# Rounds of 512 columns for Q, K and V in a recurrent segment loop, with the heads laid out anew and longer rows for the streamed weights

## The chip, the cores and the metric

The kernel runs on one core of one Trainium2 chip. The metric is the device time of the whole program in microseconds, as the median of repeated runs. The kernel before took 1744.48 us, the median of three runs between 1734.66 and 1751.12.

A core has several engines that run their own instruction lists side by side and wait for each other by semaphores: TensorE (PE) multiplies matrices, VectorE (DVE) and ScalarE (ACT) copy and compute element by element, GpSimd (POOL) does a few odd jobs, and SyncE (SP) only issues DMA transfers here. PE's results land in PSUM and have to be copied from there to the main on-chip memory (SBUF) before PE can use them again.

## The reference

Two attention layers read sequences of 2048 tokens with 640 features, and a gate mixes their results. Layer A goes through the sequence in 64 segments of 32 tokens. Eight memory rows are put in front of each segment, and the first eight rows of a segment's result are the memory of the next one, so the segments can't run side by side.

```python
n_seg = S // seg_len                      # 2048 / 32 = 64
L = M + seg_len                           # 8 + 32 = 40
mask = (idx[:, None] < M) | (idx[:, None] >= idx[None, :])
mem = mem0
for s in range(n_seg):
    xs = x[:, s * seg_len:(s + 1) * seg_len, :].copy()
    h = jnp.concatenate([mem, xs], axis=1)            # 40 x 640
    q = jnp.einsum('btd,dhe->bhte', h, Wq)            # 32 heads of 192
    k = jnp.einsum('btd,dhe->bhte', h, Wk)
    v = jnp.einsum('btd,dhe->bhte', h, Wv)
    scores = jnp.einsum('bhqe,bhke->bhqk', q, k) * scale
    scores = jnp.where(mask[None, None], scores, -1000000000.0)
    p = _softmax(scores, axis=-1)
    o = jnp.einsum('bhqk,bhke->bhqe', p, v)
    o = jnp.einsum('bhte,hed->btd', o, Wo)
    mem = o[:, :M, :].copy()
    outs.append(o[:, M:, :])
```

Layer B is a local attention of 32 heads of 20 features, in which each position sees eight positions at distances 0, 2, ... 14. The result is `g * a + (1 - g) * b` with `g = sigmoid(x . gate_w)`. All data are bfloat16. The four weights of A have 640 x 6144 elements each, 7.9 MB, 31.5 MB in all; they are read again in each segment, and not all of them fit in SBUF.

## The kernel before

**Stages.** Layer B comes first (0 to about 178 us of the span); its result lies in DRAM until it is mixed in. A pre-pass follows (178 to 357 us): the last eight rows of each segment depend on no memory, so Q, K and V of these 512 rows (called z in the code) are computed for all segments at once (`project_qk`, four passes p = 0 to 3: two of Q, two of K; then `project_v`) and stored in `zpk_dram`. The segment loop (357 to 1689 us) then has 32 rows per segment: eight memory rows and 24 rows of x. A tail, `part_z` (1689 to 1747 us), multiplies the z rows of all segments by Wo.

**One segment.** `hT` holds the segment's 640 features in five chunks (`kc`) of 128 partitions, by 32 rows. PE has 128 columns of output partitions, and a matmul with 32 rows uses a strip of 32 of them, so four matmuls run at once, one in each strip j. Such four make a quad. Of the 6144 columns of Wq a round R takes 1536, four strips of 384 columns, and accumulates over kc: five quads a round, four rounds each of Q, K and V, 60 quads in all (L736 for Q and K, L838 for V).

- `m_qk(i, kcs)` issues the quads of round i, where even i are Q and odd i are K. `c_qk(i)` copies the round from PSUM to a staging slot `V[i % 4]` of the tile TZ: on ACT, but on DVE for i = 7 (L745).
- `t_qk(i)` transposes a round on PE, three transposes of 128 columns (L754), and `c_t(i)` copies them out with DVE (L761): Q into the tile ZB (`QTa`), K into free slots of ZB and TZ (`kt_runs`). One such slot shares its columns of ZB with `a4`, the tile from which the segment's result is stored to `out_dram`.
- The heads are handled in two halves h. `s_a` and `s_b` compute scores (L785, L794), `e_exp`, `e_mask`, `e_norm` and `e_recip` are the softmax: exps on ACT (four a half, L803), the mask, a matmul with `bones` that gives the sums (L817), Ln and Exp(-x) on ACT and two products on DVE.
- `m_v(R, kcs)` and `c_v(R)` project V and copy it (L845; round 1 on DVE, the others on ACT).
- `pv_half(h)` is P V, 48 small matmuls per half (L861, L866); copies on ACT and DVE bring the result of the x rows to SBUF (L872), and `c_z` the z rows (L881).
- `o_group(part, i2)` is the output projection, twelve quads for columns 0 to 383 (`oa`) and twelve for 384 to 639 (`ob`), all L902. ACT copies the sum to `whi` (L987 for `oa`, L995 for `ob`). `sel` picks the eight memory rows out of it by small matmuls (L912), and DVE writes them into the next segment's `hT` (L915). `tail` mixes in layer B's rows, which a DMA has brought to `a4`, and `store` sends `a4` to `out_dram`.

**Order.** Within the loop the instructions of PE, ACT and DVE run in the order in which the code issues them (`tc.manual_schedule`). DMAs are issued on two queues: SP's carries all weights, ACT's the segment's small loads and stores (`load_z`, `load_vz`, `load_seg`, a4, `out_dram`, `oz_dram`), between ACT's own instructions. So a DMA that waits on a queue holds up what stands behind it.

**Weights.** They are cut into 80 slices of 384 KB (128 partitions x 1536 columns): a slice of Q, K or V is one (round, kc). 66 slices are loaded once, during layer B, the pre-pass and the first segment (`wres`, `wlate`), and stay in SBUF. 14 are read again in each segment by SP into five buffers (`wstream`, tile `wst`); `weights_setup` picks them from a list of times so that their uses are spread over the segment, Q, K, V and the output part alike. The slices of Wq, Wk and Wv come from the input tensors in rows of 3072 bytes; three of the output's come from a copy in DRAM, `wscr`.

Of the kernel before, what the change touches and what calls it, by code (L numbers as in the profile page):

```python
# [10 lines left out]
BF = mybir.dt.bfloat16  # L11
# [3 lines left out]
N_STREAM = 14  # L15
N_EARLY = 20
# [4 lines left out]
WBUFS = 5  # L21
# [6 lines left out]
class _K:  # L28
# [463 lines left out]
    def slice_keys(self):  # L492
        keys = []
        for R in range(4):
            keys += [("q", R, kc) for kc in range(self.KC)] + [("k", R, kc) for kc in range(self.KC)]
        for R in range(4):
            keys += [("v", R, kc) for kc in range(self.KC)]
        keys += [("oa", i) for i in range(12)] + [("ob", i) for i in range(8)]
        return keys

    def slice_info(self, key):

        if key[0] in ("oa", "ob"):
            Wov = self.Wo.rearrange("(c p) f -> p c f", p=128)
            n, f0, f1 = (4, 0, 384) if key[0] == "oa" else (6, 384, 640)
            return Wov[:, n * key[1]:n * key[1] + n, f0:f1], (n, f1 - f0)
        W = {"q": self.Wq, "k": self.Wk, "v": self.Wv}[key[0]].rearrange("(c p) f -> p c f", p=128)
        return W[:, key[2], key[1] * 1536:(key[1] + 1) * 1536], None

    def weights_setup(self):  # L510
        nc, tc = self.nc, self.tc
        keys = self.slice_keys()
        gap = {("q", 0, 0): 300, ("k", 0, 1): 160, ("k", 0, 3): 70, ("q", 2, 2): 900, ("v", 0, 0): 1700, ("v", 2, 0): 800,
               ("v", 3, 0): 550, ("oa", 0): 150, ("oa", 6): 1200}
        at, t = {}, 0
        for k in keys:
            t += gap.get(k, 0)
            at[k] = t
            t += 163
        self.stream_keys = set()  # L520
        for i in range(N_STREAM):
            left = [k for k in keys if k not in self.stream_keys]
            self.stream_keys.add(min(left, key=lambda k: abs(at[k] - (i + 0.5) * t / N_STREAM)))
        rest = [k for k in keys if k not in self.stream_keys]
        use = [(m, R) for m in "qkv" for R in range(4)]
# [23 lines left out]
    def load_slice(self, pool, key, name, tag=None, t=None):  # L549
        src = self.slice_info(key)[0]  # L550
        if t is None:
            t = pool.tile([128, 1536], BF, name=name, **({"tag": tag} if tag else {}))
            self.load_slice(pool, key, name, tag, t)
            return self.slice_view(key, t)
# [574 lines left out]
```

## Time and profile before

| | before |
|---|---|
| median of three runs | 1744.48 us |
| profiled execution | 1748.69 us, its span 1747.0 us |
| mean granted PE clock | 0.983 |
| segment, mean of 64 | 20.74 us |
| DMA over the span | 477.57 MB, 273 GB/s; queue q1 (weights) 415.76 MB, q10 (ACT's) 56.46 MB, q8 (instructions) 4.75 MB |
| wst loads, 384 KB each | 325 from Wv, 260 from Wk, 192 from wscr, 130 from Wq |

The profile shows one execution. "Busy" is the time in which an engine worked on an instruction; PE is its matmuls, PEld its weight loads, which run beside them. A line such as "L745 ACT CAST TZ<-ps_qk 128x384 bf16<-128x384 f32 x448 | 208.0, 479" is a group of equal instructions: source line, engine, operation, destination and source with partitions x elements and type, how many there were, the busy time of all in us and the mean of one in ns. After the second bar stands the engine's idle time just ahead of them, and what ended most of it. In the chain of waits, the work that ended last is followed back from the end, each step to what released it; "issue" there is time in which the engine waited for nothing that the profile shows. In the timeline a row has the start and the length in us, the engine, line, operation and count, and in brackets the idle time ahead of it.

### The profile page before, as it was taken

To read this page: it belongs to the slowest core of one execution; us is meant where nothing else is said; L and a number is where in the kernel's file an instruction comes from. 1 tells how busy PE (TensorE), PEld (TensorE's weight loads), DVE (VectorE), ACT (ScalarE), POOL (GpSimd) and SP (SyncE) were. 2 spreads that over 40 slices of the span, in tenths; PEclk is the share of its full clock that TensorE was granted. 3 is DMA by queue.
4 is the path that set the end of the run, shared out by engine and by line. 5 is a ranking of instruction groups with operands and counts; after the bars stand their busy time and mean duration, and the time that the engine had idled before them with its cause. 6 is when DMAs were issued, how large, how long until landed. Compare 5 with 4: busy or idle time off the path is not lost.

```text
span 1747.0 us, 83365 instructions
## 1 busy us (share of the span) xinstructions
PE 1603.0 (92%) x37049; PEld 1012.7 (58%) x37049; DVE 632.1 (36%) x2095; ACT 873.1 (50%) x2338; POOL 60.0 (3%) x124
## 2 busy tenths in 40 slices
PE   7887999889999999999998999999999999999989
PEld 4544544356565566666665666666665566666657
DVE  3765333233333333333333333333333333333320
ACT  3887322245554455555554555545555555555550
POOL 2030000000000000000000000000000000000000
PEclk9998899999999999999999999999999999999999
DMA  7897895989898898899998888988998888888881
GB/s 198 210 238 172 277 270 162 267 277 307 291 297 282 279 295 288 296 305 306 309 292 274 288 292 300 303 287 292 310 306 295 294 295 299 291 292 291 297 280 31
DMA packets 299702, 477.57 MB, mean 273 GB/s; under 512 B 100172, under 2 KB 176460, under 8 KB 299340
## 3 DMA queue, kind: packets, MB, share of 16 engines
q1 hardware_dynamic: 200208, 415.76, 73.4%
q10 hardware_dynamic: 99132, 56.46, 11.1%
q8 instruction: 290, 4.75, 1.1%
q14 instruction: 72, 0.59, 0.1%
HBM read 430.40 MB, written 44.48 MB: 272 GB/s over the span
## 4 chain that ended last, share of the span: by engine, by line
PE 74%; ACT 9%; DMA 8%; issue 5%; ACTq 2%; DVE 1%; SPq 1%; DVEq 0%
PE ps_qk L736 23%; PE ps_v L838 10%; PE ps_wo L902 9%; PE ps_pre L603 6%; PE ps_qkT L754 5%; PE ps_S L785 4%; PE ps_oT L861 3%; PE ps_z L1060 3%; PE ps_pre L617 3%; DMA out_dram<-ZB 2%; ACT TZ L845 2%; PE ps_bqk L234 2%; ACT ZB L987 2%; ACT TZ L872 1%; PE ps_mem L912 1%
## 5 line engine op out<-in xcount | busy, mean ns | idle before, releaser
L736 PEld LDWEIGHTS <-hT 128*32 128x32 bf16 x10240 | 265.7, 96 | 156.0 <-issue 19.8
L745 ACT CAST TZ<-ps_qk 128x384 bf16<-128x384 f32 x448 | 208.0, 479 | 270.8 <-PE ps_qk L736 267.7
L736 PE MATMUL ps_qk<-wres_q,hT 128*32 128x384 bf16 x4608 | 259.5, 329 | 5.0 <-issue 3.3
L736 PE MATMUL ps_qk<-wlate_k,hT 128*32 128x384 bf16 x3584 | 235.3, 327 | 2.2 <-issue 1.8
L838 PE MATMUL ps_v<-wlate_v,hT 128*32 128x384 bf16 x3840 | 208.8, 329 | 0.2 <-issue 0.2
L902 PEld LDWEIGHTS <-TZ 128*32 128x32 bf16 x6144 | 160.1, 97 | 81.8 <-issue 42.0
L761 DVE COPY ZB<-ps_qkT 128x384 bf16<-128x384 bf16 x256 | 90.6, 354 | 212.5 <-PE ps_qkT L754 212.5
L902 PE MATMUL ps_wo<-wlate_oa,TZ 128*32 128x384 bf16 x2560 | 150.2, 333 | 11.8 <-issue 10.7
L838 PEld LDWEIGHTS <-hT 128*32 128x32 bf16 x5120 | 114.9, 96 | 65.7 <-issue 7.7
L902 PE MATMUL ps_wo<-wlate_ob,TZ 128*32 128x256 bf16 x2688 | 129.0, 279 | 14.3 <-issue 14.2
L736 PE MATMUL ps_qk<-wst,hT 128*32 128x384 bf16 x1536 | 132.6, 328 | 4.4 <-issue 3.3
L803 ACT ACTIVATE TZ<-ps_S 32x224 bf16<-32x224 f32 x256 | 89.0, 348 | 75.5 <-PE ps_S L794 71.4
L838 PE MATMUL ps_v<-wst,hT 128*32 128x384 bf16 x1280 | 108.7, 329 | 6.3 <-DMA wst<-in_A_Wv_dram 6.3
L872 DVE CAST TZ<-ps_oT 128x192 bf16<-128x192 f32 x256 | 79.4, 351 | 83.8 <-PE ps_oT L866 83.7
L803 ACT ACTIVATE ZB<-ps_S 32x224 bf16<-32x224 f32 x256 | 89.0, 348 | 38.8 <-PE ps_S L794 36.6
L872 ACT CAST TZ<-ps_oT 128x192 bf16<-128x192 f32 x256 | 69.6, 327 | 76.8 <-PE ps_oT L866 76.8
L754 PE MATMUL ps_qkT<-ident,TZ 128*128 128x128 bf16 x1536 | 107.7, 219 | 0.1
L915 DVE CAST hT<-ps_mem 128x24 bf16<-128x24 f32 x126 | 22.5, 179 | 223.4 <-PE ps_mem L912 223.4
L845 ACT CAST TZ<-ps_v 128x384 bf16<-128x384 f32 x192 | 92.4, 481 | 17.4 <-PE ps_v L838 15.7
L754 PEld LDWEIGHTS <-TZ 128*128 128x128 bf16 x1536 | 88.7, 98 | 20.6 <-issue 20.6
L861 PEld LDWEIGHTS <-TZ 32*128 32x128 bf16 (+1 forms) x4096 | 48.1, 97 | 75.6 <-issue 27.0
L713 POOL COPY TZ<-ZB 128x384 bf16<-128x384 bf16 x64 | 32.6, 510 | 1515.2 <-DMA ZB<-zpk_dram 717.0
(139 smaller groups left out, 2312.9 us busy)
## 6 DMA issues: line engine op xcount, KB each, us to landing
wst<-in_A_Wv_dram SPq DMA_DIRECT2D x325, 384.0 KB
wst<-in_A_Wk_dram SPq DMA_DIRECT2D x260, 384.0 KB
wst<-wscr SPq DMA_DIRECT2D x192, 384.0 KB
wst<-in_A_Wq_dram SPq DMA_DIRECT2D x130, 384.0 KB
zpk_dram<-ZS ACTq DMA_DIRECT2D x4, 3072.0 KB
ZB<-zpk_dram ACTq DMA_DIRECT2D x64, 192.0 KB
wres_q<-in_A_Wq_dram SPq DMA_DIRECT2D x18, 384.0 KB
zpk_dram<-ZV ACTq DMA_DIRECT2D x32, 192.0 KB
```

The source lines that it names most:

```text
L603: nc.tensor.matmul(ps[:], lhsT=sls[r][kc][:, c0:c0 + 128], rhs=zTi[:, kc, :], start=(kc == 0), stop=(kc == KC - 1))
L736: nc.tensor.matmul(pq[32 * j:32 * j + 32, 0:384], lhsT=hT[:, kc, :], rhs=sl[:, 384 * j:384 * j + 384], start=(kc == 0), stop=(kc == KC - 1 ...
L745: cp(sts[i], pqs[i][:, 0:384])
L754: nc.tensor.transpose(pT[:, t, :, :, :].rearrange("p j b i -> p (j b i)"), st[:, 128 * t:128 * t + 128], self.ident[:])
L761: nc.vector.tensor_copy(q_blocks(R)[:, 1:5, :, :].rearrange("p b c i -> p c b i"), pT.rearrange("p t j b i -> p (t j) b i"))
L785: nc.tensor.matmul(grid(h, par)[:, :, 0:80].rearrange("p j (b r i) -> p j b r i", r=2, i=8)[:, :, :, r, :], lhsT=KTs[R][t][k0:k1, :], rhs= ...
L803: nc.scalar.activation(E[ps], pSs[h][ps, :, 112 * j:112 * j + 112], ACT.Exp, scale=scale_a)
L838: nc.tensor.matmul(pvs[R][32 * j:32 * j + 32, 0:384], lhsT=hT[:, kc, :], rhs=sl[:, 384 * j:384 * j + 384], start=(kc == 0), stop=(kc == KC ...
L845: cp(V[R], pvs[R][:, 0:384])
L861: nc.tensor.matmul(out[:, r, t, :], lhsT=V[2 * h + r][ks, f0:f1], rhs=E[ks, par, 0:80].rearrange("p (b r i) -> p b r i", r=2, i=8)[:, :, r ...
L872: cps[j % 2](oTxs[2 * h + j // 2][:, 6 * (j % 2):6 * (j % 2) + 6, :], pos[j][:, 0:240].rearrange("p (c q) -> p c q", q=40)[:, :, 8:40])
L902: nc.tensor.matmul(pso[part][32 * jj:32 * jj + 32, 0:n], lhsT=oTxs[2 * (R // 2) + j // 2][:, 6 * (j % 2) + 3 * (R % 2) + t, :], rhs=o_weig ...
```

## The change

Q, K and V go in three rounds u of 512 columns per strip instead of four of 384. The heads are laid out so that strip J holds the same eight heads in all rounds: the 1536 columns from 1536 J on, in twelve chunks of 128. A resident tile is now one (matrix, strip J, kc) with the rounds that are not streamed (`units`, `tile_of`, `res`). A streamed unit is one (matrix, round, kc) for all four strips: 128 partitions x 2048 columns, 512 KB, of which eleven are listed by hand (`STREAM`): four of Q, three of K and four of V, none of the output part. All of them are copied to `wscr` in DRAM first, four on SP's queue in layer B (`N_COPY`), seven at the start of the third pass of `project_qk`, and are read from there in rows of 4096 bytes, into four buffers.

In the loop there are 45 quads of 512 columns instead of 60 of 384, and the sum of copies falls: six of Q and K on ACT, three of V, all on DVE. A fourth staging slot, the new tile XB, and new slots for transposed K (`k_runs`) follow from the new shape; none of these shares columns with `a4` any more. Transposes are 24 a segment as before, four a round. The copies of transposed Q and K are split where a round crosses the two halves of heads (`parts`). The softmax's reciprocal is in two pieces (`e_recip_a` on ACT, `e_recip_b` on DVE), P V's copies are their own step (`c_x`), and the order of the steps from the first normalisation to the output is new. `o_group` goes through the chunks in a new order, `order`, such that the first six groups need only the first half of heads; the six groups that remain of each part are issued without interleaving. The load of `a4` is issued after the second P V's copies instead of before the first output group. In the tail, `load_oz` brings each fourth of the data in two halves into tiles that hold two rounds, and `sort_oz` sorts it from there.

The diff, cut to what is named here:

```diff
-N_STREAM = 14
-N_EARLY = 20
+STREAM = (("q", 0, 1), ("k", 0, 0), ("q", 0, 3), ("k", 0, 3), ("q", 2, 0), ("q", 2, 4), ("k", 2, 1), ("v", 0, 0),
+          ("v", 0, 3), ("v", 1, 1), ("v", 1, 4))
+N_EARLY = 25
+N_COPY = 4
...
-WBUFS = 5
+WBUFS = 4
...
+    def units(self, m, kc):
+        return [u for u in range(3) if (m, u, kc) not in STREAM]
...
+        self.wscr = dict(zip(STREAM, self.dram.tile([len(STREAM), 128, 2048], BF, name="wscr")))
...
+    def res(self, m, J, kc, c0, n):
+        f0 = 512 * self.units(m, kc).index(c0 // 512) + c0 % 512
+        return self.res_tiles[m, J, kc][:, f0:f0 + n]
+
+    def load_unit(self, key):
+
+        m, u, kc = key
+        t = self.wstream.tile([128, 2048], BF, name="wst", tag="wst")
+        self.nc.sync.dma_start(t[:].rearrange("p (j f) -> p j f", j=4), self.unit_src(key))
+        return t
+
+    def unit_src(self, key):
+        m, u, kc = key
+        return self.W[m][:, kc, :].rearrange("p (j f) -> p j f", j=4)[:, :, 512 * u:512 * u + 512]
+
+    def copy_unit(self, key):
+        self.nc.sync.dma_start(self.wscr[key].rearrange("p (j f) -> p j f", j=4), self.unit_src(key))
+
+    def get_unit(self, key):
+        if key in self.ahead:
+            return self.ahead.pop(key)
+        t = self.wstream.tile([128, 2048], BF, name="wst", tag="wst")
+        self.nc.sync.dma_start(t[:], self.wscr[key])
+        return t
...
+        loads = [lambda k=k: self.load_res(k, self.tile_of(self.wres, k)) for k in self.early]
+        self.pre_q = {}
+        loads += [lambda k=k: self.pre_q.update({k: self.load_unit(k)})
+                  for k in sorted(STREAM, key=lambda k: k[1]) if k[0] == "q"]
+        loads += [lambda k=k: self.copy_unit(k) for k in STREAM[:N_COPY]]
...
+            sts = {k: self.pre_q[k] if m == "q" else self.load_unit(k) for k in STREAM if k[0] == m and k[1] == 2 * Rp}
...
+            if p == 2:
+                for k in STREAM[N_COPY:]:
+                    self.copy_unit(k)
...
+        def load_v(J):
+            t = self.wstream.tile([128, 2048], BF, name="wst", tag="wst")
+            for x, (m, u, kc) in enumerate(vkeys):
+                nc.sync.dma_start(t[:, 512 * x:512 * x + 512],
+                                  self.W["v"][:, kc, 1536 * J + 512 * u:1536 * J + 512 * u + 512])
+            return t
...
+        for k in STREAM[:WBUFS]:
+            self.ahead[k] = self.get_unit(k)
...
+            XB = pers.tile([128, 512], BF, name="XB")
             V = [self.TZ[:, 384 * f:384 * f + 384] for f in range(4)]
+            VU = [self.TZ[:, 512 * u:512 * u + 512] for u in range(3)]
+            stage = VU + [XB[:]]
...
+            k_runs = ([(0, 4, XB[:])], [(0, 2, self.TZ[:, 1920:2176]), (2, 4, ZB[:, 0:256])], [(0, 4, VU[2])])
+            q_runs = ([(0, 4, 2, 0)], [(0, 2, 2, 16), (2, 4, 1, 0)], [(0, 4, 1, 8)])
...
+                def project(ps, m, u, kcs):
+                    for kc in kcs:
+                        st = self.get_unit((m, u, kc)) if (m, u, kc) in STREAM else None
+                        for j in range(4):
+                            rhs = self.res(m, j, kc, 512 * u, 512) if st is None else st[:, 512 * j:512 * j + 512]
+                            nc.tensor.matmul(ps[32 * j:32 * j + 32, :], lhsT=hT[:, kc, :], rhs=rhs, start=(kc == 0),
+                                             stop=(kc == KC - 1), tile_position=(0, 32 * j), skip_group_check=True)
...
+                    sts[i] = stage[i % 4]
+                    nc.scalar.copy(sts[i], pqs[i][:])
...
+                def c_t(i, parts=(0, 1)):
+                    u, pT = i // 2, pTs[i]
+                    for x, run in enumerate((q_runs if i % 2 == 0 else k_runs)[u]):
+                        if x not in parts:
+                            continue
+                        src = pT[:, 128 * run[0]:128 * run[1]]
+                        if i % 2 == 0:
+                            n = 4 * (run[1] - run[0])
+                            nc.vector.tensor_copy(
+                                QTf[:, run[2]:run[2] + 4, run[3]:run[3] + n, :].rearrange("p b x i -> p x b i"),
+                                src.rearrange("p (x b i) -> p x b i", b=4, i=8))
+                        else:
+                            nc.vector.tensor_copy(run[2], src)
...
+                def e_recip_a(h):
+                    rz = pSs[h][:, 0, 0:160].rearrange("p (a f) -> p a f", a=2)
+                    nc.scalar.activation(rz, rz, ACT.Ln)
+                    nc.scalar.activation(rz, rz, ACT.Exp, scale=-1.0)
+
+                def e_recip_b(h):
                     E = Es[h]
                     EA, EB = E[:, :, 0:80], E[:, :, 80:112]
-                    pz = pSs[h][:, 0, 0:160].rearrange("p (a f) -> p a f", a=2)
...
+                def c_v(u):
+                    nc.vector.tensor_copy(VU[u], pvs[u][:])
...
+                def c_x(h, pos, js, engs):
+                    for j, eng in zip(js, engs):
+                        cp = nc.scalar.copy if eng == "a" else nc.vector.tensor_copy
+                        cp(oTxs[2 * h + j // 2][:, 6 * (j % 2):6 * (j % 2) + 6, :],
+                           pos[j][:, 0:240].rearrange("p (c q) -> p c q", q=40)[:, :, 8:40])
...
+                osl = {(part, i): self.res_tiles[part, i] for part, n in (("oa", 12), ("ob", 8)) for i in range(n)}
+                order = [12 * J + x for x0 in (0, 6) for J in (0, 1, 3, 2) for x in range(x0, x0 + 6)]
...
-                for i in range(4):
-                    c_t(i)
+                c_t(0); c_t(1)
+                c_t(2, (0,)); c_t(3, (0,))
+                c_t(3, (1,))
                 m_qk(4, (2, 3, 4)); c_qk(4)
-                m_qk(5, range(KC)); c_qk(5)
...
+                m_qk(5, range(KC)); c_qk(5)
                 s_a(0, HALF); s_a(1, HALF); s_b(0, HALF)
                 s_a(0, FULL); s_a(1, FULL); s_b(0, FULL)
                 e_exp(0)
-                for i in range(4, 8):
-                    t_qk(i)
+                t_qk(4); t_qk(5)
+                c_t(2, (1,))
                 c_t(4); c_t(5)
                 e_mask(0)
-                c_t(6); c_t(7)
-                m_v(0); c_v(0)
+                m_v(0)
+                c_v(0)
...
-                m_v(1, (0, 1, 2))
-                e_norm(0); e_recip(0)
-                m_v(1, (3, 4)); c_v(1)
+                m_v(1, (0,))
+                e_norm(0); e_recip_a(0); e_recip_b(0)
                 s_a(2, HALF); s_a(3, HALF); s_b(1, HALF)
                 s_a(2, FULL); s_a(3, FULL); s_b(1, FULL)
                 e_exp(1)
-                m_v(2); c_v(2)
+                m_v(1, (1, 2, 3, 4)); c_v(1)
                 e_mask(1)
+                m_v(2, (0, 1, 2))
                 pos = pv_half(0)
-                m_v(3, (0, 1, 2))
-                c_z(0, pos, (1, 3), "dd")
-                m_v(3, (3, 4))
-                e_norm(1); e_recip(1)
-                c_v(3)
-                c_z(0, pos, (0, 2), "aa")
-                nc.scalar.dma_start(a4[:], self.bsc_dram[32 * s:32 * s + 32, :].rearrange("t (j f) -> j t f", j=4))
+                c_x(0, pos, (0, 1, 3), "add")
+                e_norm(1)
+                e_recip_a(1)
+                m_v(2, (3, 4)); c_v(2)
+                e_recip_b(1)
+                c_x(0, pos, (2,), "a")
+                c_z(0, pos, (1, 3), "aa")
+                c_z(0, pos, (0, 2), "dd")
                 for i2 in range(6):
                     o_group("oa", i2)
                 pos = pv_half(1)
+                c_x(1, pos, range(4), "adda")
+                nc.scalar.dma_start(a4[:], self.bsc_dram[32 * s:32 * s + 32, :].rearrange("t (j f) -> j t f", j=4))
                 c_z(1, pos, range(4), "adad")
                 nc.scalar.dma_start(self.oz_dram[s], zst)
...
-                for i2 in range(5):
+                for i2 in range(6):
                     o_group("ob", i2)
-                for i2 in (6, 9, 7, 10, 8, 11):
+                for i2 in range(6, 12):
                     o_group("oa", i2)
                 nc.scalar.copy(whi[:, 0:384], pso["oa"][:, 0:384])
                 if s + 1 < nseg:
                     load_z(s + 1)
                     pm = psS.tile([128, 2, 512], F32, tag="S", name="ps_mem")
-                for i2 in range(5, 12):
+                for i2 in range(6, 12):
                     o_group("ob", i2)
                     if i2 == 8 and s + 1 < nseg:
                         sel("oa", hT_next, pm)
...
```

## The prediction

> **What bounds the kernel now.** I read the page first, for the shares and the chain.
>
> ```profile
> span 1747.0 us, 83365 instructions
> ...
> PE 1603.0 (92%) x37049; PEld 1012.7 (58%) x37049; DVE 632.1 (36%) x2095; ACT 873.1 (50%) x2338; POOL 60.0 (3%) x124
> ...
> PE 74%; ACT 9%; DMA 8%; issue 5%; ACTq 2%; DVE 1%; SPq 1%; DVEq 0%
> ```
>
> TensorE (PE) is busy for 92% and carries 74% of the chain. The 5% "issue" is time in which it waited for nothing that the profile names. Next, the windows: the segment loop, 64 segments from 357 to 1689 us.
>
> ```profile
> 357.00:1689.00 1332.00, 1232.33 (x32304) 804.85 (x32304) 470.18 (x1795) 692.86 (x2051) 32.10 (x63) 0.99 0.90 296
> ```
>
> After the length come busy time of PE, weight loads, DVE, ACT and POOL, then clock, DMA share and GB/s. PE and the DMA engines (0.90) are both close to full; DVE and ACT are not. A segment takes 20.74 us (mean distance of the 64 ACT copies of L995). The groups give the unit prices.
>
> ```profile
> L736 PE MATMUL ps_qk<-wres_q,hT 128*32 128x384 bf16 x4608 | 259.5, 329 | 5.0 <-issue 3.3 <-ACT TZ L745 1.6
> L745 ACT CAST TZ<-ps_qk 128x384 bf16<-128x384 f32 x448 | 208.0, 479 | 270.8 <-PE ps_qk L736 267.7 <-DMA wst<-in_A_Wv_dram 3.1
> L845 DVE CAST TZ<-ps_v 128x384 bf16<-128x384 f32 x64 | 35.3, 551 | 4.3 <-PE ps_v L838 4.3
> L79 DVE CAST ZV<-ps_pre 128x512 bf16<-128x512 f32 x24 | 15.8, 688 | 42.5 <-PE ps_pre L617 23.1 <-issue 10.8 <-DMA wlate_oa<-in_A_Wo_dram 8.6
> ```
>
> Last, the timeline of PE in one late segment.
>
> ```profile
> 1263.99 0.34 PE L838 MATMUL ps_v<-wst,hT 128*32 128x384 bf16 x4
> 1264.26 0.27 PE L861 MATMUL ps_oT<-TZ 32*128 32x40 bf16 x16
> ...
> 1265.38 0.34 PE L838 MATMUL ps_v<-wst,hT 128*32 128x384 bf16 x4
> 1265.55 0.27 PE L817 MATMUL ps_S<-ZB,bones 128*32 128x160 bf16 x8
> 1265.69 1.05 PE L902 MATMUL ps_wo<-wlate_oa,TZ 128*32 128x384 bf16 x20
> 1266.51 0.39 PE L902 MATMUL ps_wo<-wst,TZ 128*32 128x384 bf16 x4
> 1267.19 0.28 PE L861 MATMUL ps_oT<-ZB,TZ 32*128 32x40 bf16 x16 [0.29 <-ACT TZ L881]
> ...
> 1269.48 0.27 PE L902 MATMUL ps_wo<-wlate_ob,TZ 128*32 128x256 bf16 x1
> 1270.16 0.39 PE L902 MATMUL ps_wo<-wlate_ob,TZ 128*32 128x256 bf16 x5 [0.41 <-issue]
> ```
>
> Two idle stretches are to be seen. The first, before the second P V, is a wait on copies; it comes in nearly every segment (start to start 617 ns in the median, 270 where nothing waits: 0.35 us). The second has no cause in the program. I numbered PE's records (weight loads and matmuls) in order of time: of the 62 pauses over 0.64 us in the loop, 57 fall on numbers that leave 193 to 195 when divided by 256. They come with the 16 KB packets of queue q8 (256 instructions of 64 bytes), and PE resumes about 2.3 us after the start of such a packet. So they are fetches of PE's own instructions. They cost 1.29 us a segment over 61 segments, 82 us in all.
>
> **Part by part, per segment.** *Q, K, V.* Four matmuls run together, one in each 32-column strip. Such a quad of 384 columns takes 163 ns (5 quads from 1253.27 to 1254.08), so 0.425 ns a column; 512 columns make 217, as in the pre-pass (120 matmuls of 512 columns in 26.07 us at L603). Before: 60 x 163 = 9.78; after: 45 x 217 = 9.77. Nothing, between -0.1 and +0.1. Transposes stay 24.
>
> *Round copies.* Eight copies of Q and K (479 to 556 ns) become six on ACT at about 586 (L77, 512 columns); each has a whole round of 1.09 us as cover, so they cost nothing. If a cover failed, each would cost some 0.3. The three V copies all go to DVE at 688 ns, and there one is uncovered: V round 1 ends, DVE starts 0.29 later (as at 1259.13 to 1259.42 in the trace), copies 0.69, and 0.05 passes to PE: 1.03 us. In front of the first P V stand only three quads of round 2 and the 0.10 of a change of array shape, 0.75. Wait: 0.28. On PE everything else is queued behind it.
>
> *First normalisation.* It needs the mask, which needs the exps: 0.2 + 4 x 0.357 + 0.03 + 0.28 + 0.05 = 1.99 us after the scores. PE has eight transposes (0.54) and six quads (1.30) before it: wait 0.15. Before, twelve transposes and eight quads (2.07) covered it.
>
> *From P V to P V.* Before 2.93 us (1264.26 to 1267.19), with the 0.35 wait. After: P V 0.44, sums 0.11, two quads 0.43, then V round 2's copy 0.29 + 0.69, the two products 0.40 and 0.05: 2.41, with 0.34 of idle in it. Three quads (0.49) have moved ahead of it. The old wait is replaced, not removed: 0.
>
> *Output.* Between the first part's last group and `sel` stand three groups of 256 columns instead of four: the copy L987 (0.48) loses 0.11 of cover. One change of array shape less: -0.1. ACT's load of a4 is issued 2.6 us later; what waits for it is the DVE sum in the next segment, 4 us on, with the transposed copies behind it: nothing, unless that DMA takes over 4 us.
>
> *Out store.* The second half of K's copy no longer lands in the a4 columns, so the wait on the `out_dram` store goes: in rows 2.9 us (PE, L785) and 7.7 (weight loads), over the loop. I take 4.
>
> Waits together: +0.28 + 0.15 + 0 + 0.11 - 0.1 = +0.44; a second sum, block by block along both segments, gives +0.36. I take the lower one, as it counts shared starts once: 64 x 0.36 = +23 us (+10 to +38).
>
> *Instruction fetch.* PE's records fall from 1012 to 892 a segment, so 3.95 blocks of 256 become 3.48. In the rows with a pause, 4.4 to 5.5 us pass from a block's first record to the next block's. A block of Q, K, V quads took 128 x 41 ns = 5.2 us and will take 128 x 54 = 6.9: never late. Blocks around both P V (192 records in under 1 us) take about 3.2 us before, 2.8 after, since the two P V stand closer. Walking a window of 256 records along both segments with a need of 4.6 us gives 1.29 before (as measured) and 0.96 after: -0.33, -21 us (0 to -45).
> The Trainium skill (Runtime: NRT & Kernel Launch, "Instruction fetch mechanics") agrees on blocks of 16 KiB and 256 instructions, but says that the fetch is hidden because dispatch is slower. The trace disagrees, with the 1.29 us above. By the page this term would be 0 and the time 21 us higher.
>
> *Stream.* 14 slices of 384 KB become 11 of 512 KB: 5.51 to 5.77 MB. In the packet records a 3,072-byte packet has a median of 121 ns, 1,536 bytes 65, 768 bytes 36; the line gives 158 for 4,096. Stream work per DMA engine: 14 x 8 x 121 = 13.6 us before, 11 x 8 x 158 = 13.9 after. But all 11 uses now lie between the first Q round and V's round 1, the last 12.5 us after the segment's start, and only four buffers run ahead. Seven loads must follow each other from 0.7 (the first buffer free, seen by SP) plus 1.0 to the first packet. At 350 GB/s (queue 1 with all 16 engines on it) a load takes 1.5: the last arrives at 12.2. At 330 it takes 1.6, and arrives at 12.9. The lowest spacing by packets alone (1.27) gives 10.6. Between these the last unit is 0.3 early or 0.4 late, and arrivals scatter: I take a mean wait of 0.15 in place of none: +10 us (0 to +50).
>
> *Outside the loop.* Part B's queue carries 11.4 MB instead of 10.1, eleven copies to scratch among them, and K's two streamed units are issued on SP behind 39 late loads (before 30, of the same 11.5 MB), where a store of ZS held SP for 17.7 us. K's pass can start late by 3 to 5 us: +5 (0 to +12). The end's transfers keep their bytes.
>
> Sum on the span: 1747.0 + 23 - 4 - 21 + 10 + 5 = 1760, +13. That execution took 1748.7 us, 1.7 over its span and 4.2 over the median of the runs shown, 1744.5. On the median: 1757.
>
> **Rivals.** *Stream becomes the bound (slower).* Place: V's units. If a load takes 1.7 (where loads were issued in a backlog, the packets show 1.31 per 384 KB; times 158/121), the seventh arrives at 13.6, 1.1 after its use: 0.95 a segment more than above, 1757 + 61 = 1818. It decides from about 1.55 us a load. For: DMA share 0.90 already. Against: SP nearly always waited for a buffer, not for data, and PE lost under 2 us to `wst` between 420 and 1660 us. Chance 0.18.
> *Fetch gains more, waits less (faster).* If blocks need only 4.2 us, little over the dense stretch's own time, pauses fall to 0.5 a segment (-50 us instead of -21), and with the stream on time and waits at their low end (+10): 1744.5 - 50 + 10 - 4 + 5 = 1706. For: every Q, K, V block is now far from its limit. Against: the pauses of before sit in P V and output, where the blocks get denser. Chance 0.29.
> *Pauses stay (slower).* If the dense stretch keeps its one pause a segment, as it has one boundary in nearly every segment, the -21 fall away: 1757 + 21 = 1778. This is also what the page's rule gives; 0.03 of the chance is for it, 0.08 for the denser stretch: 0.11.
> The forecast keeps 0.42.
>
> **Numbers.** About 1% (17 us) is what can be told from no change here. Within the forecast's own case (1735 to 1785, by the waits' bounds and the stream up to 1.55 us a load) I give within 1% 0.32 and slower 0.10. With the faster rival 0.28 fast and 0.01 within, the slower two 0.28 and 0.01: faster 0.28, same 0.34, slower 0.38. The range for 8 in 10 reaches from the faster rival to the stream rival: 1705 to 1815.
>
> **What would show it.** L756 quads at 217 ns; gaps before the first P V (0.28) and the sums (0.15), ended by DVE; "issue" gaps at P V and output, 256 records apart, near 1 us a segment; PE waits on `wst` at V under 0.3 a segment. Wrong if quads of 512 columns take over 220 ns, if DVE's copies are not what PE waits for, or if V's units are late by a microsecond.

## The result: 8% slower, and the profile after

The changed kernel took 1888.2 us (median of 4 runs, 1873.7 to 1896.4) beside 1744.4 us (median of 4, 1734.7 to 1751.1): a ratio of 1.082, 95% interval 1.0735 to 1.0905. That is above the range given (1705 to 1815). The profiled execution took 1885.7 us, its span is 1884.0, 137 more than before. The page, with PE's busy time and the chain of waits:

```profile
span 1884.0 us, 75241 instructions
...
PE 1646.7 (87%) x33209; PEld 899.9 (48%) x33209; DVE 695.1 (37%) x2103; ACT 804.9 (43%) x2090; POOL 59.8 (3%) x124
...
PE 51%; DMA 40%; issue 4%; ACT 2%; DVE 1%; SPq 1%; ACTq 0%; DVEq 0%
DMA wst<-wscr 34%; PE ps_wo L916 12%; PE ps_qk L756 9%; PE ps_v L756 7%; PE ps_pre L608 6%; PE ps_oT L881 3%; PE ps_z L1081 3%; PE ps_pre L638 2%; PE ps_S L810 1%; DMA bqkT<-bqk_dram 1%; ACT ZB L1006 1%; PE ps_bqk L236 1%; PE ps_mem L927 1%; PE ps_qkT L777 1%; PE ps_S L842 1%
```

Of the chain, 40% is now DMA, before 8%. Nearly all of that is one line, the streamed weights (34% of the span). The stretch of the loop, columns as in the prediction:

```profile
365.00:1827.00 1462.00, 1273.02 (x28467) 690.63 (x28460) 533.34 (x1803) 623.74 (x1795) 31.95 (x63) 0.98 0.81 281
```

The loop is 130 us longer and PE is busy for 87% of it in place of 93%. The DMA engines, the busiest after PE before, have fallen from 0.90 to 0.81, though PE now waits for them. The groups that the prediction priced (name, busy time and mean, then the idle time ahead):

```profile
L756 PE MATMUL ps_qk<-w_k,hT 128*32 128x512 bf16 x3072 | 235.7, 382 | 0.0
L756 PE MATMUL ps_qk<-wst,hT 128*32 128x512 bf16 x1792 | 178.3, 385 | 59.4 <-DMA wst<-wscr 57.8
L865 DVE CAST TZ<-ps_v 128x512 bf16<-128x512 f32 x192 | 132.8, 692 | 102.5 <-PE ps_v L756 102.2
L756 PE MATMUL ps_v<-wst,hT 128*32 128x512 bf16 x1024 | 103.1, 391 | 47.3 <-DMA wst<-wscr 45.4
L916 PE MATMUL ps_wo<-w_ob,TZ 128*32 128x256 bf16 x3072 | 131.1, 283 | 35.4 <-issue 34.4
```

Resident weights cost no idle time; streamed ones do. The same within one segment, on PE's timeline (the counterpart of the one before):

```profile
1262.30 0.28 PE L819 MATMUL ps_S<-ZB,TZ 128*128 128x128 bf16 x2
1263.09 0.40 PE L756 MATMUL ps_v<-wst,hT 128*32 128x512 bf16 x4 [0.51 <-DMA wst<-wscr]
1263.30 0.62 PE L756 MATMUL ps_v<-w_v,hT 128*32 128x512 bf16 x8
1264.34 0.40 PE L756 MATMUL ps_v<-wst,hT 128*32 128x512 bf16 x4 [0.42 <-DMA wst<-wscr]
1264.56 0.83 PE L756 MATMUL ps_v<-w_v,hT 128*32 128x512 bf16 x12
1265.32 0.41 PE L881 MATMUL ps_oT<-TZ 32*128 32x40 bf16 x16
...
1268.27 0.72 PE L916 MATMUL ps_wo<-w_ob,TZ 128*32 128x256 bf16 x18
1271.55 0.40 PE L916 MATMUL ps_wo<-w_ob,TZ 128*32 128x256 bf16 x6 [2.56 <-issue]
```

V's round 1 waits twice for a unit. The first P V follows with no wait. In the output part, one pause for instructions takes 2.56 us. Now the same segment in stretches of 3 us; the last two columns are the busy share of the DMA engines and GB/s:

```profile
1253.50:1256.50 3.00, 2.88 (x52) 1.42 (x45) 0.00 (x0) 1.37 (x3) 0.00 (x0) 1.00 1.04 408
1256.50:1259.50 3.00, 3.00 (x52) 1.59 (x49) 1.44 (x5) 1.11 (x2) 0.00 (x0) 1.00 1.03 386
1259.50:1262.50 3.00, 3.00 (x55) 1.85 (x53) 1.94 (x5) 2.03 (x7) 0.00 (x0) 1.00 0.96 314
1262.50:1265.50 3.00, 2.06 (x42) 0.92 (x40) 1.17 (x4) 1.39 (x4) 0.00 (x0) 1.00 1.01 376
1265.50:1268.50 3.00, 2.99 (x146) 1.74 (x138) 2.05 (x9) 1.25 (x7) 0.00 (x0) 1.00 0.95 386
1268.50:1271.50 3.00, 0.49 (x18) 0.21 (x7) 0.91 (x4) 0.84 (x4) 0.00 (x0) 1.00 0.24 78
1271.50:1274.50 3.00, 2.71 (x69) 2.07 (x72) 0.18 (x1) 0.77 (x2) 0.00 (x0) 1.00 0.14 28
```

From 1253.5 to 1268.5 the DMA engines are full, then for 6 us they are almost idle: the stream works in bursts. Before, no such stretch of the segment that I looked at was under 0.89; the lowest was this one, in the output part:

```profile
1268.00:1271.00 3.00, 2.59 (x73) 1.49 (x62) 0.90 (x5) 1.12 (x5) 0.00 (x0) 1.00 0.89 285
```

The loads show why. From the records of packets, issues and matmuls, medians over some 55 segments, in us from the first use of the first unit (the last column is the use in a segment without stalls, from the run after_noreload below):

```
unit     issued  last packet  used   used, no stalls
q 0 1    -11.5      -7.6       0.0       0.0
k 0 0    -10.8      -5.8       0.4       0.4
q 0 3     -8.9      -4.5       1.4       1.4
k 0 3     -7.7      -2.1       1.9       1.9
q 2 0      0.4       3.5       4.5       4.5
q 2 4      0.9       5.4       6.5       6.4
k 2 1      1.9       6.8       8.1       6.9
v 0 0      2.4       8.2      10.3       9.1
v 0 3      4.9       9.9      11.1       9.7
v 1 1      6.9      11.4      12.9      11.5
v 1 4      8.6      13.1      14.0      12.2
```

The first four units fill the four buffers 4 to 8 us before they are used and wait there for the next segment, since nothing in the output part is streamed any more. The other seven can only be issued from then on, and run one behind another, some 1.6 us from end to end (3.5 to 13.1 in six steps). In 167 cases the first quad of a unit began over 0.4 us after the matmul ahead of it, so that PE was waiting; it then began 1.32 us after the load's last packet in the median (middle half 0.89 to 1.64).

Per segment, from the distances between starts of PE's matmuls, place by place, over 61 and 62 segments: pauses for instructions are those over 0.3 us above the median at block boundaries, "wst" the excess at the first quad of a streamed unit. Both hold to about 0.2, by what is taken as the base.

| us per segment | before | after |
|---|---|---|
| mean | 20.66 | 22.61 |
| wait for wst | 0.17 | 2.13 |
| pauses for instructions | 1.12 | 1.24 |
| rest | 19.37 | 19.24 |

So the 137 us are 63 distances of segments, 22.736 in place of 20.742 (+125.6, the last segment's stall included), the time to the first segment's last copy (395.0 in place of 382.2, +12.9) and the rest after the last one (-1.5).

### The profile page after: what moved, and what is told of

It is laid out like the page before. It is cut to its first block, busy times and chain, and to the rows that moved or that the text cites. A ratio compares the mean times of both kernels' runs of the same rounds, so it can differ in the third digit from the quotient of the medians.

```text
span 1884.0 us, 75241 instructions
## 1 busy us (share of the span) xinstructions
PE 1646.7 (87%) x33209; PEld 899.9 (48%) x33209; DVE 695.1 (37%) x2103; ACT 804.9 (43%) x2090; POOL 59.8 (3%) x124
## 4 chain that ended last, share of the span: by engine, by line
PE 51%; DMA 40%; issue 4%; ACT 2%; DVE 1%; SPq 1%; ACTq 0%; DVEq 0%
DMA wst<-wscr 34%; PE ps_wo L916 12%; PE ps_qk L756 9%; PE ps_v L756 7%; PE ps_pre L608 6%; PE ps_oT L881 3%; PE ps_z L1081 3%; PE ps_pre L638 2%; PE ps_S L810 1%; DMA bqkT<-bqk_dram 1%; ACT ZB L1006 1%; PE ps_bqk L236 1%; PE ps_mem L927 1%; PE ps_qkT L777 1%; PE ps_S L842 1%
## 5 line engine op out<-in xcount | busy, mean ns | idle before, releaser
L756 PEld LDWEIGHTS <-hT 128*32 128x32 bf16 x11520 | 281.1, 96 | 407.3 <-issue 151.0
L769 ACT CAST TZ<-ps_qk 128x512 bf16<-128x512 f32 x320 | 181.2, 587 | 360.1 <-PE ps_qk L756 348.9
L756 PE MATMUL ps_qk<-w_k,hT 128*32 128x512 bf16 x3072 | 235.7, 382 | 0.0
L756 PE MATMUL ps_qk<-wst,hT 128*32 128x512 bf16 x1792 | 178.3, 385 | 59.4 <-DMA wst<-wscr 57.8
L756 PE MATMUL ps_qk<-w_q,hT 128*32 128x512 bf16 x2816 | 223.2, 384 | 1.6 <-issue 0.8
L756 PE MATMUL ps_v<-w_v,hT 128*32 128x512 bf16 x2816 | 211.2, 383 | 0.0
L916 PE MATMUL ps_wo<-w_oa,TZ 128*32 128x384 bf16 x3072 | 163.3, 336 | 11.5 <-issue 10.8
L865 DVE CAST TZ<-ps_v 128x512 bf16<-128x512 f32 x192 | 132.8, 692 | 102.5 <-PE ps_v L756 102.2
L916 PE MATMUL ps_wo<-w_ob,TZ 128*32 128x256 bf16 x3072 | 131.1, 283 | 35.4 <-issue 34.4
L756 PE MATMUL ps_v<-wst,hT 128*32 128x512 bf16 x1024 | 103.1, 391 | 47.3 <-DMA wst<-wscr 45.4
```

The source lines that it names most:

```text
L756: nc.tensor.matmul(ps[32 * j:32 * j + 32, :], lhsT=hT[:, kc, :], rhs=rhs, start=(kc == 0), stop=(kc == KC - 1), tile_position=(0, 32 * j), ...
L769: nc.scalar.copy(sts[i], pqs[i][:])
L865: nc.vector.tensor_copy(VU[u], pvs[u][:])
L916: nc.tensor.matmul(pso[part][32 * jj:32 * jj + 32, 0:n], lhsT=oTxs[2 * (g // 2) + J // 2][:, 6 * (J % 2) + 3 * (g % 2) + t, :], rhs=osl[pa ...
```

## The experiments

The theory: what is streamed is bunched. Eleven uses lie within 12 us, four buffers run ahead, the DMA engines idle in between. Rivals, some with a letter in the texts below: the bytes alone are too many; the new order itself waits on copies; fixed delays of a load and not its bytes; pauses for instructions. The runs at a glance, the two columns on the right found as above:

| run | us, median | ratio to before (95%) | wst | pauses |
|---|---|---|---|---|
| changed kernel | 1888 | 1.082 (1.0735-1.0905) | 2.13 | 1.24 |
| after_noreload | 1669 | 0.959 (0.949-0.968) | 0 | 0.05 |
| before_noreload2 | 1655 | 0.947 (0.938-0.957) | 0 | 0.01 |
| after_half | 1686 | 0.968 (0.959-0.977) | 0.03 | 0.17 |
| before_half | 1663 | 0.952 (0.943-0.962) | 0.01 | 0.10 |
| after_rows1024 | 1948 | 1.119 (1.108-1.129) | 3.4 | 1.07 |
| before_qkv | 1863 | 1.067 (1.056-1.077) | 2.5 | 0.15 |
| before_4buf | 1788 | 1.023 (1.015-1.031) | 1.3 | 0.72 |
| after_spread | 1755 | 1.007 (1.003-1.011) | 0.9 | 0.44 |
| after_spread2 | 1876 | 1.072 (1.064-1.079) | 2.4 | 0.30 |
| after_spread2_oz | 1867 | 1.069 (1.062-1.076) | 2.3 | 0.28 |
| after_spread3 | 1787 | 1.026 (1.020-1.032) | 1.2 | 0.71 |

**The stream taken away.** The units loaded ahead stay in their buffers.

```diff
-        if key in self.ahead:
-            return self.ahead.pop(key)
+        if len(self.ahead) == WBUFS:
+            return self.ahead[STREAM[STREAM.index(key) % WBUFS]]
```

> The changed kernel, but the four units loaded ahead of the loop stay in their four buffers and stand for all eleven streamed units in every segment; no weight is read again in the loop. Theory A (bunched stream): the wait on wst, 2.1 us a segment, is the whole loss, and nothing else waits in its place. A segment falls from 22.7 to 20.4 (19.2 without any stall, 1.24 of instruction fetch), the time to 1745 (1740 to 1755). Theory B (the new order itself waits on copies, and the stream only covers it): waits of DVE and ACT appear in place of wst, 0.4 us or more a segment, and the time stays over 1770. If pauses for instructions are long because weights share the DMA engines, they shrink too, and the time goes below 1720.

1669 us, less than any theory's main number. PE's idle groups, by line and releaser:

```profile
PE ps_mem L927 <- ACT ZB L1006: 16.8, 63, 0.6
PE ps_z L1081 <- ACT ZB L1006: 9.6, 1, 9.6
```

These two are the longest that are left: us, times, longest. Neither wst nor "issue" is among them. The order itself is not the loss (theory B falls), and the pauses for instructions left with the weights, which the last sentence had as a possibility.

The kernel before, with the same edit, was to be the counterpart. Fewer than five slices are loaded ahead there, so its condition never held and the stream ran on: 1738.0 us, a ratio of 1.000 (0.995 to 1.005), the kernel before once more.

> The kernel before, with the same left out: the five slices loaded ahead of the loop stand for all fourteen streamed ones. It gives the change without its stream. By the forecast's other terms (+23 of waits on copies, -4, -21 of instruction fetch, +5 outside the loop) the changed kernel without reloads is 3 us above this one. By the trace of the changed kernel (waits on copies 0, fetch 0, outside the loop +13) it is 13 above. By theory B it is 40 or more above. Its own time: 1730 to 1745, since PE lost almost nothing to wst before; below 1710 if the pauses for instructions come from sharing the DMA engines with weights.

The second try loads five slices into a list and serves all uses from it:

```diff
+        if self.fixed:
+            keys = [k for k in self.slice_keys() if k in self.stream_keys]
+            return self.slice_view(key, self.fixed[keys.index(key) % WBUFS])
...
+        self.fixed = [self.get_slice(k) for k in [k for k in self.slice_keys() if k in self.stream_keys][:WBUFS]]
```

> The kernel before without reloads, with the edit that takes hold: the first five streamed slices are loaded once and stand for all fourteen in every segment. The changed kernel without reloads lost its pauses for instructions (0.06 us a segment in place of about 1.2). Theory C (the pauses come from sharing the DMA engines with weights) says the same here: 1744 less 64 x 1.29 (pauses) less 64 x 0.17 (wst) = 1651 (1640 to 1665), so the changed kernel's 1669 without reloads is 13 to 25 above it. If the pauses belong to the order of PE's instructions, they stay here, and the time stays over 1720. The forecast's terms for waits on copies (+23, -4) and outside the loop (+5) put the changed kernel 24 above this one; the trace's (0 and +13) put it 13 above.

1655, 1651 expected, and the changed kernel without reloads is 15 above it, between the trace's 13 and the forecast's 24. The two together split the result: the stream costs the changed kernel 1888 - 1669 = 219 us and the kernel before 1744 - 1655 = 90. The difference, 129, is nearly all of the 144. All other edits cost 15; some 6 of these are the last segment (28.0 us in place of 22.1, see the account of the prediction).

**Half the bytes, same loads.**

```diff
-        self.nc.sync.dma_start(t[:], self.wscr[key])
+        self.nc.sync.dma_start(t[:, 0:1024], self.wscr[key][:, 0:1024])
...
-rhs = self.res(m, j, kc, 512 * u, 512) if st is None else st[:, 512 * j:512 * j + 512]
+rhs = self.res(m, j, kc, 512 * u, 512) if st is None else st[:, 512 * (j % 2):512 * (j % 2) + 512]
```

> The changed kernel with streamed loads of half the size: only the first 1024 columns of a unit are loaded (256 KB, rows of 2048 bytes), and strips 2 and 3 use the weights of strips 0 and 1. Same number of loads, same buffers, same places of use. If the loads wait for bytes (1.63 us from one end to the next in a backlog, nearly all of it transfer), the spacing falls to about 0.85, the seventh load comes 5 us earlier, and the time falls to about 1755. If a load's fixed delays (1 to 2.5 us from issue to its first packet, 1.3 from its last packet to PE) decide, the spacing stays over 1.3 and at least half of the wait of 2.1 us a segment remains: over 1815.

1686: the wait is gone, so it is the transfers behind one another that are late, and not the fixed delay of each load, which a chain of loads pays only once. It went below the 1755 expected because the pauses shrank too. In the kernel before, with 768 of 1536 columns:

> The kernel before with streamed loads of half the size (192 KB; rows of 1536 bytes, or half the rows of an output slice), and strips 2 and 3 using the weights of strips 0 and 1. Theory C: the pauses for instructions fall from 1.1 to under 0.4 us a segment, and the time to 1665 to 1690, beside 1686 for the changed kernel with half its bytes. If the pauses need the stream to be off altogether, it stays over 1700.

1663, just under the 1665 to 1690 expected.

**Rows of 1024 bytes again.** `get_unit` returns `self.load_unit(key)`, which reads the weights themselves.

> The changed kernel, with the streamed units read from the weights themselves, in four rows of 1024 bytes per partition, and not from the copy with rows of 4096. A packet of 1024 bytes took 46 ns in the pre-pass, so 184 for 4096 bytes in place of 159. If the stream's bytes are the bound between V's units, the spacing goes from 1.63 to 1.88 us, seven loads in a row cost 1.75 us a segment, and the time is about 2000. If fixed delays are the bound, the time stays within 20 us of 1888.

1948: +60, half of the 112 expected, and more than fixed delays would give. The long rows are a gain of some 60 us for this kernel; without them the change would be worse.

**Bunching alone, in the kernel before.**

```diff
-            left = [k for k in keys if k not in self.stream_keys]
+            left = [k for k in keys if k not in self.stream_keys and k[0] in ("q", "k", "v")]
```

> The kernel before, with its fourteen streamed slices chosen among Q, K and V alone: none of the output part. Same bytes, five buffers, same rows. Theory A: the nine loads after the first five follow each other at 1.42 us, plus 1 us to the first packet and 1.3 after the last: 15.1 us for V's last slices, which are used about 13.5 us after the segment's start. Some 1.6 us of wait a segment, so 1845 (1800 to 1870). If the place of the uses doesn't matter, the time stays at 1744.

The selection puts three V slices in place of the three output slices, so that four of the five slices of V's last round are streamed. 1863, within the range. PE's longest wait:

```profile
PE ps_v L838 <- DMA wst<-in_A_Wv_dram: 134.8, 155, 2.4
```

It was 6.3 us in the kernel before. With bytes, rows, buffers, rounds and order of the kernel before, the place of three uses alone costs 117 us. The bunching is shown, independent of the rest of the change. That the time met its range is in part luck: the wait is longer than the 1.6 us expected, and the pauses, taken as unchanged, fell from 1.12 to 0.15. And the 117 are not all waiting. The loop's window, with the granted clock third from the end:

```profile
365.00:1805.00 1440.00, 1272.35 (x32179) 802.34 (x32179) 467.62 (x1789) 689.99 (x2044) 31.95 (x63) 0.96 0.84 273
```

PE is busy for 1272 us of the loop, before for 1232, at a granted clock of 0.96 in place of 0.99. The clock records have 34 stretches of mostly 3.4 us at half the clock in this loop and 6 in the kernel before. Ahead of each, PE had been idle for 1.5 us or more of the last 3.4 us, elsewhere for 0.3 to 0.4 in the mean. Matmul by matmul they cost 0.56 us a segment in place of 0.11, some 29 of the 117 us. In the changed kernel there are 11 (0.24 us a segment, some 8 of the 144 us), in after_spread2 22 (0.50), in the loops without a stream none or one.

**One buffer less, in the kernel before** (`WBUFS = 4`).

> The kernel before with four stream buffers in place of five. Its loads end 2.2 to 4.2 us before their use (median by place), and PE needs about 1.3 of that. One buffer less puts off each issue by one distance of uses, 1.3 to 1.5 us, so the tightest places come late: 0.3 to 0.8 us of wait a segment, 1775 (1755 to 1800). If only the places of the uses matter and not the buffers, 1745.

1788, within the range, with 1.3 us of wait a segment in place of the 0.3 to 0.8 expected, and shorter pauses (0.72, before 1.12). Buffers count too; the change took one away and made each a third larger.

**The uses spread in the changed kernel.** Output slices can be streamed here too, by a few lines in `get_unit`, `copy_unit` and `o_group`; what differs is the list:

```diff
+STREAM = (("q", 0, 1), ("q", 0, 3), ("q", 2, 0), ("q", 2, 2), ("k", 2, 2), ("v", 0, 0), ("v", 0, 2), ("v", 1, 3),
+          ("v", 2, 4), ("oa", 6), ("oa", 5), ("ob", 7))
```

> The changed kernel with another list of streamed units: two units of K and none of V less, three slices of the output part more (two of oa, one of ob, 384 KB each), and the units of Q, K and V chosen so that the twelve uses lie 0.7 to 2.6 us apart over the whole segment. Four buffers as before, 5.90 MB a segment in place of 5.77, rows of 4096 and 3072 bytes from the copy. Theory A (eleven uses bunched in 14 of 20 us, four buffers): every use is now at least 5.5 us after the use that frees its buffer, a load takes 4 to 5, so the wait on wst falls from 2.1 to 0.2 to 0.5 us a segment, pauses for instructions stay at 1.2, and the time is about 1775 (1755 to 1800). Theory D (5.8 MB in four buffers are too much in any order): the wait stays over 1.2 us a segment, and the time over 1830.

1755, 133 under the changed kernel with 2% more bytes, and 0.7% over the kernel before. It lies at the edge of its range by two errors that cancel: the wait is 0.9 in place of 0.2 to 0.5, the pauses are 0.44 in place of 1.2. PE's two longest waits for a unit:

```profile
PE ps_v L765 <- DMA wst<-wscr: 39.6, 57, 5.2
PE ps_qk L765 <- DMA wst<-wscr: 9.7, 17, 1.4
```

They stood at 45.4 and 57.8 on the page after, and those figures leave out the time booked ahead of PE's weight loads. This answers theory D: the bytes fit, if the uses are placed for it. Three attempts to do better all missed:

```diff
+STREAM = (("q", 0, 2), ("q", 0, 4), ("q", 2, 0), ("q", 2, 1), ("k", 2, 3), ("v", 0, 0), ("v", 1, 1), ("v", 2, 2),
+          ("oa", 3), ("ob", 6), ("oa", 2), ("ob", 7))
```

> The changed kernel with exactly its bytes per segment (5.77 MB), in another list: four units of Q, one of K and three of V (eight of 512 KB), and four slices of the output part (two of oa, two of ob, 384 KB each), with uses 1.2 to 2.6 us apart almost everywhere. A replay of SP's queue with the figures of the traces (a load is issued when the use four places before it is over, 1.0 us to the first packet, 1.7 us from end to end for 512 KB and 1.33 for 384, 1.15 from the last packet to PE) gives 2.4 us of wait a segment for the changed kernel, 0.7 for after_spread (measured 2.1 and 0.9), and 0.0 here. Theory A: the wait falls to 0.0 to 0.3, pauses for instructions stay at the 0.45 of after_spread, and the time is 1755 - 64 x 0.7 = 1710 (1695 to 1730), under the kernel before. Theory D (bytes alone count): with the bytes of the changed kernel the wait stays near 0.9 or above, and the time over 1745.

1876 in place of 1710. Its time alone would be theory D's, but after_spread streams more bytes and waits 0.9, so the bytes alone don't decide. The waits are at q 0 4 (about 1.5 us a segment) and its neighbours (0.3 each). The buffer of q 0 4 comes free only 4.1 us ahead of it, at the end of the output part, where the small loads of ACT's queue run as well: the load of q 0 2 took 3.4 us from first to last packet. The replay had neither.

> after_spread2, and in the last segment SP issues four weight loads ahead of the eight 192 KB loads of oz (load_oz(0)) in place of behind them. In the changed kernel and in after_spread one V unit of the last segment came late by 5 to 7 us behind these loads. If that is its cause, the last segment's 27 us fall to about 21 and the time by 5 us against after_spread2 (3 to 7); if the loads of oz are then late for the tail, the time is the same.

9 us under after_spread2, and its last segment took 26.8 us in place of 27.6: the 5 us are not shown, the two runs differ by about their scatter.

```diff
+STREAM = (("q", 0, 1), ("k", 0, 4), ("q", 2, 0), ("q", 2, 2), ("q", 2, 3), ("v", 0, 0), ("v", 0, 4), ("v", 1, 3),
+          ("v", 2, 2), ("oa", 6), ("ob", 4), ("ob", 7))
```

> The changed kernel with a fourth list: five units of Q and K, four of V, three output slices (the bytes of after_spread, 5.90 MB), and the last segment's order of after_spread2_oz. after_spread2 missed its forecast: its waits sit at Q's kc 4 and kc 2 of the first round. Theory A2: what counts is the distance, in a segment without stalls (the quads' times of after_noreload), from the end of a use to the use four places later, since the buffer freed by the one is what the other needs; a load takes 4 to 4.8 us from issue to its last packet under load and 1.3 more to PE, so places with under about 5.3 us are late. The changed kernel has five of them (4.25, 4.87, 5.06, 5.10, 5.22), after_spread2 four (4.10, 4.50, 4.88, 5.02, the first two where its waits are), after_spread three (4.84, 4.94, 5.23), this one one (5.27). By A2 the wait falls to 0.2 to 0.5 us a segment, the pauses for instructions stay near 0.45, and the time is 1755 - 64 x 0.5 - 5 = 1718 (1700 to 1735). If bytes in flight or the loads on ACT's queue at the segment's start decide and not the distances, it is no better than after_spread: 1745 or more.

1787 in place of 1718, so distances to the freeing use alone (theory A2) don't decide. Here it is the second of two close uses that is late: q 2 3 follows q 2 2 by 0.24 us, but its load ends 1.4 us later, and PE waits 0.46 a segment there; v 2 2, 0.9 behind v 1 3, waits 0.2 to 0.4. A list has to hold both, distance and spacing, and ACT's loads as well. Which list would beat the kernel before stays open; none that ran did.

## Why the prediction was wrong

**The stream, the step that failed.** Forecast 0.15 us a segment, measured 2.13 - 0.17 = 1.96, or 125 us in place of 10. The chain of seven loads was the right mechanism, and "the last arrives at 12.2" to 12.9 counted to the last packet. What was missing is the 1.3 us from there to PE. The trace of before shows them as a floor: its loads ended 2.3 to 4.2 us ahead of their use in the median by place, and never under 1.2; I took all of this for slack. With it, and 1.6 us a load, the forecast's slower bound: 0.7 + 1.0 + 7 x 1.6 + 1.3 = 14.2, against a use at 12.5; 1.7 late, near the 1.96 that were measured. The Trainium skill (DMA: Bandwidth & Descriptors, "Anatomy of one DMA — SWDGE (gpsimd) path") says so for another issuing path: about 2 us fixed per DMA, most of it until the last byte is confirmed as landed and the semaphore can fire. The 1.3 us after the last packet and 1.0 ahead of the first, where the queue was empty, agree with it in sum.

**The rival was there, with its price too low.** It was to decide from about 1.55 us a load, and 1.6 is just beyond that; it gave 1818 for want of the same 1.3 us (with them 1901). The argument against it, that SP nearly always waited for a buffer and not for data, was misread: a queue that waits for buffers while the DMA engines idle is what bunching looks like.

**Instruction fetch.** Forecast -0.33, measured +0.12, or -0.12 if every excess over 0.3 us outside the first quads of streamed units is counted (1.31 and 1.19): about nothing, and the rival "pauses stay" was right. There are fewer pauses (0.8 a segment in place of 1.05), but the gap is longer each time (1.6 in place of 1.2 us), as the paused blocks take some 3.4 us of their own in place of 3.7. The step that failed took the 4.6 us between blocks as PE's need. It is the loaded queue's: ahead of a pause, a block's packet started 2.5 us after the block before began. Over all blocks it was 1.9 us in the kernel before and 1.8 in the changed one, 0.9 in both with half the stream, and 0.4 to 0.5 without, where the pauses are gone.

**Waits on copies.** Forecast +0.36. Without the stream, the sums of the medians are 19.21 and 19.14 us: +0.07. The 0.28 ahead of the first P V is not there. Its first twelve products read V's round 0 only; on the timeline they start at 1265.32, and DVE's copy of round 1 runs from 1264.79 to 1265.48:

```profile
1264.79 0.69 DVE L865 CAST TZ<-ps_v 128x512 bf16<-128x512 f32 x1 [1.80 <-PE ps_v L756]
```

A part of it comes inside the P V: without the stream, the thirteenth product starts 0.148 us behind the twelfth, in the second P V 0.015. From P V to P V it is 2.48 us all the same, where 2.41 was forecast. The other two terms hold without the stream: the first half's sums wait 0.14 us (0.15 forecast; 0.07 with the stream), and from the last group to `sel` it is 0.53 us in place of 0.42, the 0.11 forecast. So the term was too high by its first part. DVE's wait on the `out_dram` store, 92.9 us over the run before, is gone, as forecast.

**Outside the loop.** Forecast +5 (0 to 12), measured 12.9 - 1.5. K's pass did start late, by 4.9 us on the Wk unit, and a V unit of the first segment by 5.0 (3.0 before). Inside the loop, the last segment took 30.8 us (25.7 before): a V unit came 6.6 us late (3.3 before), with the loads of oz issued ahead of it on SP. I had not looked there, and after_spread2_oz does not show that these are the cause. The stream is not all of it: after_noreload's last segment still took 28.0 us (22.1 in before_noreload2). There the profile puts 7.1 us of ACT's idle time down to `w_k<-oz_dram`, ACT's copies for `sort_oz` come ahead of those of the sum, and PE stands still for 9.6 us, as the second row of that run's idle groups shows.

**Prices.** 512-column quads start 216 ns apart, 217 forecast; DVE's copies took 692 ns (688), ACT's 587 (586).

On the span: stream 64 x (1.96 - 0.15) = 116 more than forecast, fetch 64 x 0.45 = 29 more, waits 64 x 0.29 = 19 less, outside 6 more. That makes 132, beside the 124 between the forecast's 1760 and the 1884 measured.

## What to carry to other kernels

Price a stream that runs ahead by its buffers and by the places of its uses, not by its share of the DMA engines: for each use, the time since its buffer came free, against the full time from issue to the consumer's start (here 4.4 to 7.1 us: 3.1 to 5.8 from issue to the last packet by the table above, 1.3 after), and no uses closer together than one transfer. Of the lists made by parts of this rule none beat the kernel before, so it is a check for lateness and not a recipe. Fewer and larger loads leave fewer buffers in the same memory, and a part of the loop without any use lets them run full and the DMA engines idle. A falling DMA share beside growing DMA waits is the sign.

## What the runs showed of the hardware that I had not expected

PE's own instruction fetch suffers from the weights on the DMA engines: 1.1 to 1.2 us of pauses a segment with the full stream, 0.10 to 0.17 with half its bytes, 0.01 to 0.05 with none, in both kernels. So the Trainium skill's sentence that the fetch is hidden (Runtime: NRT & Kernel Launch, "Instruction fetch mechanics") agrees with the runs without the stream, and not with those with it. Other lists of the same bytes gave 0.15 to 0.71; what decides between these is not settled.

After its longer waits PE also runs slower for a while: stretches of 3.4 us at half the granted clock followed where PE had been idle for 1.5 us or more in 3.4 (34 of them in before_qkv, 0 or 1 in the loops without a stream).
